# A seventh matmul of 128 rows in place of 96 in the gate/up products of a transformer block

## The chip, the cores and the metric

The kernel runs on one core of a Trainium2 chip. A core has a matrix engine (TensorE, PE in the profile, with its weight loads listed as PEld), a vector engine (DVE), a scalar engine (ACT), a general engine (POOL) and SyncE (SP), which here issues transfers. They run side by side and wait for each other by semaphores. The on-chip memory and the accumulator banks (PSUM) that TensorE writes both have 128 rows (partitions). A matmul takes a stationary operand of up to 128 rows by 128 columns, loaded first, and a moving operand of the same rows and up to 512 columns; the rows are what is summed over. The metric is the time of one execution on the device, in microseconds (us); lower is better.

## The reference

A transformer block on 2048 tokens of width 576: conditioned layer norm, attention with 32 heads of width 18 in four segments of 512 tokens with a running memory, output projection and residual, and then a gated feed-forward part with an inner width of 4608. This case is about the feed-forward part:

```python
def _B_ref(x, w_gate, w_up, w_down):
    g = _silu(x @ w_gate)
    u = x @ w_up
    return (g * u) @ w_down
...
h = _layernorm(x, axis=-1) * (1 + cb) + sb
x = x + gb * _B_ref(h, B_w_gate, B_w_up, B_w_down)
```

## The kernel before

The first part of the kernel (to about 543 us) computes layer norm, projections and attention. The projections to queries and keys (line 576) are chains of 14 matmuls of 128 rows and 512 columns, and the projections to values behind them (line 605) have 288 columns.

The feed-forward part goes through the tokens in two halves (`t` = 0, 1) and in each half through 18 pairs of inner blocks of 128 (`p`, `NPR` = 18). Each product x @ w is made by a Strassen-like scheme: of width, inner block and tokens each halved, seven products of combined operands take the place of eight. So a pair has seven products for the gate (`z` = 0) and seven for up (`z` = 1), 14 in all, and both halves together have 504. Every operand is split into a high and a low part (F32R type), and high x high, low x high and high x low are added.

A half of the width is 288 = 128 + 128 + 32. The function `prod` (lines 1409 to 1417) therefore issues seven matmuls per product: three for each full block of 128, from the weight tiles `wh`, `wl` and the operand tile `y`, and one for the remaining 32. In this seventh one the three combinations of high and low are stacked as 3 x 32 = 96 rows, in the weight tile `R[z]` (called wr in the profile, since its tag is "wr") and in the fifth part of the operand tile, `y[0:96, o, 4]`. The operand tile has room for all seven operands of a half, 128 rows by 7 by 5 by 512.

`prep_r` (lines 1357 to 1366) fills the weight tile: in the first half ACT copies 96 rows (line 1365) and DVE subtracts the low part into rows 32 to 63 (line 1366), in two parts of three and four products; `store_r` keeps the result in memory, and in the second half one transfer brings it back (line 1362). `prep_w` (lines 1376 to 1382) makes wh on ACT and wl on DVE. Before the change the tile is taken anew from the pool `wrp` of two buffers each time, in turns for gate and up. `load_y`, `y_here` and `prep2` write rows 0 to 95 of the fifth part of `y`, never the last 32.

Results of the products gather in three kinds of PSUM banks, A, B and C (`step`), from which ACT and DVE take them (`copy_t`, `fin`). The down projection of the pair before is cut into chunks which run between the products: `down` (line 1525, six matmuls of 288 columns, 14 chunks a pair) in the second half's first 16 pairs, and `plain` (line 1544, twelve matmuls of 288 columns, eight chunks a pair) in all pairs of the first half and the last two of the second. The lists `CH` and `CH0` say at which of the 14 steps a chunk is issued: `CH` has chunks behind 12 steps (behind two of them two chunks) and none behind two, `CH0` has one behind each of eight steps and none behind six. The last eight plain chunks come after all products.

The order of all this is written out by hand: within an engine, instructions run in the order of the program. Ahead of the pairs stands the output projection's last unit (line 874, 32 steps counted by `n`), into which the first preparations are placed: POOL combines weights at steps 2 to 5 (`sum_o`, line 1371), and `prep_r` and `prep_w` stand at the steps listed in `WW`.

Of the kernel before, what the change touches and what calls it, by code (L numbers as in the profile page):

```python
# [8 lines left out]
F32R = mybir.dt.float32r  # L9
# [6 lines left out]
P = 128  # L16
# [83 lines left out]
def f32(ap):  # L100
    return ap.bitcast(F32)
# [3 lines left out]
def block(ctx: ExitStack, tc: tile.TileContext, x, wqk, wv, wo, beta, wgu, wd, c, w_mod, wm01, out):  # L105
    nc = tc.nc
    def pool(stk, name, bufs=1, **kw):
        return stk.enter_context(tc.tile_pool(name=name, bufs=bufs, reuse_waits="tile", **kw))
# [223 lines left out]
    with ExitStack() as p1:  # L332
# [90 lines left out]
        with ExitStack() as p0:  # L423
# [54 lines left out]
            for b in range(3):  # L478
                n = P if b < 2 else 64
# [93 lines left out]
        def proj(s, t):  # L573
            pp = ps.tile([P, L], F32, tag="p", name="pp", bufs=3)
            for n, (a, b) in enumerate(p_ops(s, t)):
                nc.tensor.matmul(pp, lhsT=a, rhs=b, start=(n == 0), stop=(n == 13))
            f = pb.tile([P, L], F32, tag="pf", name="pf")
            fh = pb.tile([P, L], F32R, tag="fh", name="fh")
            fl = pb.tile([P, L], F32R, tag="fl", name="fl")
            nc.scalar.copy(fh, pp)  # L580
            nc.scalar.copy(f, pp)
            nc.vector.tensor_tensor(fl, f, f32(fh), op=ALU.subtract)
            k_store(s, t, fh, fl)
            q_store(s, t, fh, fl)
            q0, q1, r = q_rows(t)
            if q1 > 0:
                if s > 0:
                    e = pb.tile([P, L], F32, tag="pq1", name="pq1")
                    nc.vector.tensor_scalar(e[r:], f[r:], 0.0, None, op0=ALU.min)
                    nc.scalar.activation(e[r:], e[r:], AF.Exp)  # L590
                    nc.vector.scalar_tensor_tensor(e[r:], f[r:], 0.0, e[r:], op0=ALU.max, op1=ALU.add)
                    nc.sync.dma_start(qF[s][q0:q1, :], e[r:])
            return f
# [39 lines left out]
        for s in range(3):  # L633
# [11 lines left out]
            for t in QKORD:  # L645
# [4 lines left out]
                f = proj(s, t)  # L650
# [188 lines left out]
    def load_xr(s, i):  # L839
        xr = o3.tile([P, D], F32, tag="xr", name="xr") if s < 3 or i in (0, 3) else xp.tile([P, D], F32, tag="xs", name="xr")  # L840
        nc.sync.dma_start(xr, x[s][:, i, :])
        return xr

    def wo_r(s, i):
        pt = ps.tile([P, 4, P], F32, tag="b" if s < 3 else "x", name="pto", bufs=8 if s < 3 else 4)
        for kt in range(4):
            nc.tensor.transpose(pt[:, kt, :], ot[s][:, i, 128 * kt:128 * kt + 128], ident)
        pto[s, i] = pt
        oh, ol = [hvp.tile([P, L], F32R, tag=f"{n}{i % 2}", name=n).rearrange("p (a b) -> p a b", b=P) for n in ("hh", "hl")]
        oT[s, i] = (oh, ol, load_xr(s, i) if s < 3 else xr3[i])  # L850

    def wo_s(s, i):
        nc.scalar.copy(oT[s, i][0], pto[s, i])

    def wo_t(s, i):
        oh, ol, _ = oT[s, i]
        nc.vector.tensor_tensor(ol, pto.pop((s, i)), f32(oh), op=ALU.subtract)
# [3 lines left out]
    def wo_m(s, i, h, c):  # L861
        oh, ol, _ = oT[s, i]
        sl = slice(288 * h, 288 * h + 288)
        if c == 0:
            wps[0] = ps.tile([P, L], F32, tag="b" if s < 3 else "w", name="pw", bufs=8 if s < 3 else 2)
        ops = []
        for k in range(4):
            ops += [(oh[:, k], woh[:, k, sl]), (oh[:, k], wol[:, k, sl]), (ol[:, k], woh[:, k, sl])]
        if s == 3:
            ops = [ops[n] for n in (0, 1, 3, 4, 6, 7, 9, 10, 2, 5, 8, 11)]  # L870
        if c == WC - 1:
            ops += [(orr[s][:, i], woh[:, 4, sl]), (orr[s][:, i], wol[:, 4, sl])]
        for n in range(14 * c // WC, 14 * (c + 1) // WC):
            nc.tensor.matmul(wps[0][:, :288], lhsT=ops[n][0], rhs=ops[n][1], start=(n == 0), stop=(n == 13))  # L874

    def wo_x(s, i, h):
        xr = oT[s, i][2]
        sl = slice(288 * h, 288 * h + 288)
        nc.vector.tensor_tensor(xr[:, sl], wps[0][:, :288], xr[:, sl], op=ALU.add)
        if h == 1:  # L880
            (nc.scalar if (s, i) == (2, 3) else nc.sync).dma_start(xD[s][:, i, :], xr)
# [252 lines left out]
    p4 = ExitStack()  # L1134
# [3 lines left out]
    SLOT = {1: 0, 2: 1, 3: 6, 4: 2, 5: 4, 6: 5, 7: 3}  # L1138
    ACT_OP = {1: 0, 2: 1, 3: 2, 4: 6, 5: 3, 6: 4, 7: 5}
# [111 lines left out]
    def y_here(j):  # L1251
        o, kb = (4, 6, 2)[j // 3], j % 3
        n = P if kb < 2 else 96
        f = ys[kb] if o == 4 else yh(1 if o == 6 else 2, kb)
        d = y[:, o, kb if kb < 2 else 4]
        nc.scalar.copy(d[:n], f[:n])
        if kb < 2:
            later.append(lambda: nc.vector.tensor_tensor(y[:, o, 2 + kb], f, f32(d), op=ALU.subtract))
        else:
            later.append(lambda: nc.vector.tensor_tensor(d[64:96], f[64:96], f32(d[64:96]), op=ALU.subtract))  # L1260
# [78 lines left out]
    O, W, R, RW, DP = {}, {}, {}, {}, {}  # L1339
    later = []  # L1340

    def flush():
        while later:
            later.pop(0)()
# [9 lines left out]
    def store_o(p, z, eng=nc.scalar):  # L1354
        eng.dma_start(oD[p][z], O[p, z][:, 3:7, 0:2])

    def prep_r(t, p, z, part=0):
        if part == 0:
            R[z] = wrp.tile([P, 7, P], F32R, tag="wr", name="wr")
        r = R[z]  # L1360
        if t == 1:
            (nc.sync if p or z == 0 else nc.scalar).dma_start(f32(r[0:96]), rD[p][z])
            return
        o, c = O[p, z], slice(0, 3) if part == 0 else slice(3, 7)
        nc.scalar.copy(r[0:96, c], o[0:96, c, 2, :])
        later.append(lambda: nc.vector.tensor_tensor(r[32:64, c], o[32:64, c, 2, :], f32(r[32:64, c]), op=ALU.subtract))

    def sum_o(p, z, j, eng=nc.gpsimd):
        o = O[p, z]
        d, a, b, op = ((4, 3, 2, ALU.add), (5, 4, 0, ALU.subtract), (3, 0, 3, ALU.subtract), (6, 1, 5, ALU.subtract))[j]  # L1370
        eng.tensor_tensor(o[:, d], o[:, a], o[:, b], op=op)  # L1371
# [4 lines left out]
    def prep_w(p, z, m):  # L1376
        o = O[p, z][:, SLOT[m], 0:2]
        wh = wp.tile([P, 2, P], F32R, tag="wh", name="wh")
        wl = wp.tile([P, 2, P], F32R, tag="wl", name="wl")
        nc.scalar.copy(wh, o)  # L1380
        later.append(lambda: nc.vector.tensor_tensor(wl, o, f32(wh), op=ALU.subtract))  # L1381
        W[z, m] = (wh, wl)
# [26 lines left out]
    def prod(z, m, bank, first):  # L1409
        wh, wl = W.pop((z, m))  # L1410
        o = ACT_OP[m]
        ops = [(wh[:, k] if a != 1 else wl[:, k], y[:, o, 2 + k if a == 2 else k])
               for k in range(2) for a in range(3)]
        ops.append((R[z][0:96, SLOT[m]], y[0:96, o, 4]))
        for n, (a, b) in enumerate(ops):
            nc.tensor.matmul(bank, lhsT=a, rhs=b, start=(first and n == 0), stop=(n == 6),  # L1416
                             skip_group_check=not first)
# [169 lines left out]
    with tc.manual_schedule():  # L1587
# [49 lines left out]
        y = yp.tile([P, 7, 5, L], F32R, tag="y", name="y")  # L1637
        tp = pool(p4, "tp")
        opl = pool(p4, "opl")
        wp = pool(p4, "wp", WR)  # L1640
        wrp = pool(p4, "wrp", 2)
        xr3 = {i: load_xr(3, i) for i in range(3)}
        p5 = ExitStack()
        ys = [hvp.tile([P, L], F32, tag="hh2", name="ys"), yt[2][:, 4, :L],
# [19 lines left out]
        for i in range(4):  # L1664
            for h in range(2):
                for c in range(WC):
                    n = 8 * i + 4 * h + c
                    wo_m(3, i, h, c)
                    if c == 3:
                        wo_x(3, i, h)  # L1670
                    flush()
                    if n in SS:
                        j = SS.index(n)
                        sum_o(0, j // 4, j % 4, nc.vector if j > 3 else nc.gpsimd)
                    if n == 24:
                        nc.scalar.activation(omg[:, 0:1], omg[:, 0:1], AF.Silu)
                        store_o(0, 0)
                    if n in HH:
                        y_here(HH.index(n))
                    if n in WW:  # L1680
                        j = WW.index(n)
                        if j < 2:
                            prep_r(0, 0, 0, j)
                        prep_w(0, 0, next(gw))
                if h == 1 and i < 2:
                    wo_r(3, i + 2)
                    wo_s(3, i + 2)
                    wo_t(3, i + 2)
# [14 lines left out]
        n, nw = 0, PF  # L1703
# [5 lines left out]
        for t in range(2):  # L1709
            for p in range(NPR):  # L1710
# [16 lines left out]
                for k in range(14):  # L1727
                    z, m = ZM[PRIME[k] if prev is None else k]
# [66 lines left out]
                    if prev is not None and is_plain(*prev):  # L1795
# [3 lines left out]
                        if CH0[t][k]:  # L1799
                            f = plain(*prev, chunk)  # L1800
# [103 lines left out]
```

## Time and profile before

| | |
|---|---|
| median of 3 runs | 1809.43 us |
| lowest and highest | 1808.07 and 1813.18 us |
| the profiled execution, first to last instruction | 1808.8 us |
| TensorE busy | 1783.9 us, 99% |
| weight loads busy | 1512.5 us, 84% |
| DVE busy | 1485.3 us, 82% |
| ACT busy | 947.8 us, 52% |
| POOL busy | 493.5 us, 27% |
| first and last start of a gate/up matmul | 543.6 and 1791.4 us |

The profile shows one execution. Of that execution no time beside its span was kept, so the median of the runs, 0.6 us above the span, stands for what lies around it. Matmuls are pipelined: the next one starts while the one before is still shown as running, and the shown ends are modelled. The distance from start to start says how long a matmul holds the engine; the shown duration is longer. In a row, "A<-y,wr 96*128 96x512" is a matmul that writes the bank A from the operand y and the weights wr, with a stationary operand of 96 rows by 128 columns and a moving one of 96 rows by 512 columns. "x288" is a count. What stands behind "<-" in a wait is what ended it.

### The profile page before, as it was taken

How to read it: one execution, taken by the hardware profiler on the slowest of the kernel's cores; microseconds unless marked ns; L12 is line 12 of the kernel's file. 1: busy time of each engine (PE TensorE's matmuls, PEld its weight loads, DVE VectorE, ACT ScalarE, POOL GpSimd, SP SyncE). 2: the span in 40 equal slices, each digit the busy share in tenths (PEclk: the TensorE clock that was granted, in tenths of full speed). 3: DMA queues.
4: the chain of work that ended last, by engine and by line, in shares of the span. 5: the costliest groups of instructions: out<-in, count | busy, mean ns of one | idle time of the engine just before them, and what ended most of it. 6: DMA issues, size and time to landing. Idle time of an engine off the chain costs nothing.

```text
span 1808.8 us, 31104 instructions
## 1 busy us (share of the span) xinstructions
PE 1783.9 (99%) x11053; PEld 1512.5 (84%) x11053; DVE 1485.3 (82%) x3278; ACT 947.8 (52%) x2073; POOL 493.5 (27%) x707
## 2 busy tenths in 40 slices
PE   8999999999999999999999999999999999999999
PEld 5888867767777888888888888888888888888888
DVE  7567589999978888889889897768888888888886
ACT  6344578778865445445544444344544544544542
POOL 2100146556661545544455444100000000000000
PEclk9999999999999999999999999999999999999999
DMA  8678766677677555456554544683324324323331
GB/s 296 225 242 281 235 200 178 173 194 217 185 236 258 174 197 173 147 169 208 170 158 141 169 147 135 199 282 130 107 80 129 107 82 128 108 82 128 107 103 53
DMA packets 178562, 304.49 MB, mean 168 GB/s; under 512 B 25304, under 2 KB 108184, under 8 KB 176616
## 3 DMA queue, kind: packets, MB, share of 16 engines
q1 hardware_dynamic: 151032, 248.66, 44.0%
q10 hardware_dynamic: 27376, 53.86, 8.5%
q8 instruction: 87, 1.43, 0.3%
q14 instruction: 67, 0.55, 0.1%
HBM read 188.42 MB, written 113.33 MB: 167 GB/s over the span
## 4 chain that ended last, share of the span: by engine, by line
PE 78%; DMA 3%; DVE 3%; POOL 1%; issue 1%; ACT 1%; ACTq 0%; SPq 0%; POOLq 0%; DVEq 0%
PE A L1416 24%; PE pd L1544 14%; PE C L1416 12%; PE pd L1525 10%; PE B L1416 6%; PE av L766 3%; PE pw L874 2%; PE s L711 2%; PE s L740 2%; PE pn L1010 1%; DMA y<-yD 1%; DVE junk L211 1%; DMA O<-in_wgu_dram 1%; DMA xD<-xr 1%; PE pw L951 1%
## 5 line engine op out<-in xcount | busy, mean ns | idle before, releaser
L1416 PE MATMUL A<-y,wh 128*128 128x512 f32 x1152 | 406.2, 393 | 2.3 <-DMA y<-yD 1.4
L1416 PEld LDWEIGHTS A<-y,wh 128*128 128x128 f32 x1152 | 216.6, 188 | 47.3 <-ACT B L1462 2.4
L1381 DVE TENSOR_TENSOR wl<-O,wh 128x256 fp32r<-128x256 f32 x504 | 246.4, 494 | 2.1 <-ACT wh L1380 1.6
L211 DVE CUSTOM_DVE_ANT_0 junk<-s,tri 128x384 bf16<-128x384 f32 (+3 forms) x512 | 218.5, 486 | 22.7 <-PE s L711 8.8
L1416 PE MATMUL A<-y,wl 128*128 128x512 f32 x576 | 226.9, 394 | 0.0
L1530 DVE TENSOR_TENSOR acc<-acc,pd 128x576 f32<-128x576 f32 x216 | 162.1, 751 | 59.2 <-PE pd L1525 51.6
L1416 PE MATMUL C<-y,wh 128*128 128x512 f32 x576 | 202.9, 393 | 1.5 <-DVE cu L1439 1.5
L1380 ACT CAST wh<-O 128x256 fp32r<-128x256 f32 x504 | 197.7, 405 | 4.9 <-DMA yD<-st 3.0
L1554 DVE TENSOR_TENSOR acc<-acc,pd 128x576 f32<-128x576 f32 x156 | 116.9, 749 | 89.0 <-PE pd L1544 88.3
L1544 PE MATMUL pd<-dh,ah 128*128 128x288 f32 x640 | 189.0, 295 | 0.5 <-DVE x L1548 0.5
L1544 PE MATMUL pd<-dh,al 128*128 128x288 f32 x640 | 189.1, 296 | 0.0
L1544 PE MATMUL pd<-dl,ah 128*128 128x288 f32 x640 | 188.8, 295 | 0.0
L1371 POOL TENSOR_TENSOR O<-O 128x384 f32<-128x384 f32 x132 | 149.4, 1145 | 142.7 <-DMA O<-in_wgu_dram 60.6
L1485 ACT CAST ah<-sg 128x512 fp32r<-128x512 f32 x192 | 119.1, 621 | 75.6 <-DVE sg L1440 69.3
L747 ACT ACTIVATE Pt<-s 128x512 f32<-128x512 f32 x256 | 135.4, 599 | 21.8 <-PE s L740 11.6
L1486 DVE TENSOR_TENSOR al<-sg,ah 128x512 fp32r<-128x512 f32 x192 | 136.3, 710 | 9.9 <-ACT ah L1485 9.7
L1525 PE MATMUL pd<-dh,ah 128*128 128x288 f32 x448 | 133.0, 297 | 0.0
L1525 PE MATMUL pd<-dh,al 128*128 128x288 f32 x448 | 132.5, 296 | 0.0
L1525 PE MATMUL pd<-dl,ah 128*128 128x288 f32 x448 | 132.3, 295 | 0.0
L1416 PEld LDWEIGHTS C<-y,wh 128*128 128x128 f32 x576 | 108.3, 188 | 22.3 <-DVE cu L1439 1.9
L1544 PEld LDWEIGHTS pd<-dl,ah 128*128 128x128 f32 x640 | 120.5, 188 | 7.2
L1544 PEld LDWEIGHTS pd<-dh,ah 128*128 128x128 f32 x640 | 120.8, 189 | 6.8 <-DVE x L1548 0.8
(412 smaller groups left out, 4337.2 us busy)
## 6 DMA issues: line engine op xcount, KB each, us to landing
O<-in_wgu_dram SPq DMA_DIRECT2D x36, 768.0 KB
O<-oD SPq DMA_DIRECT2D x36, 512.0 KB
oD<-O ACTq DMA_DIRECT2D x34, 512.0 KB
ks<-kD SPq DMA_DIRECT2D x64, 216.0 KB
qs<-qD SPq DMA_DIRECT2D x64, 216.0 KB
O<-in_wgu_dram SPq DMA_DIRECT2D x36, 384.0 KB
rD<-wr ACTq DMA_DIRECT2D x36, 336.0 KB
wr<-rD SPq DMA_DIRECT2D x35, 336.0 KB
```

Source lines behind the costliest of these rows:

```text
L211: nc.vector.tensor_tensor_reduce(junk[:, :n], bank[:, o:o + n], tri[:, L - n:], 1.0, -3e38, op0=ALU.add, op1=ALU.max, accum_out=mcol[u][0] ...
L747: nc.scalar.activation(pt[:, h], bank, AF.Exp, scale=SCALE)
L1371: eng.tensor_tensor(o[:, d], o[:, a], o[:, b], op=op)
L1380: nc.scalar.copy(wh, o)
L1381: later.append(lambda: nc.vector.tensor_tensor(wl, o, f32(wh), op=ALU.subtract))
L1416: nc.tensor.matmul(bank, lhsT=a, rhs=b, start=(first and n == 0), stop=(n == 6), skip_group_check=not first)
L1485: nc.scalar.copy(ah, src)
L1486: later.append(lambda: nc.vector.tensor_tensor(al, src, f32(ah), op=ALU.subtract))
L1525: nc.tensor.matmul(pd[:, i, :288], lhsT=a[:, tk], rhs=w, start=(k == 0), stop=(k == 2))
L1530: nc.vector.tensor_tensor(o, o, pd[:, :, :288], op=ALU.add)
L1544: nc.tensor.matmul(pd[:, i, :288], lhsT=a[:, tk], rhs=w, start=(k == 0), stop=(k == 5))
L1554: nc.vector.tensor_tensor(o, o, pd[:, :, :288], op=ALU.add)
```

## The change

The seventh matmul of a product reads all 128 rows of the weight tile and of the operand. The last 32 rows of both are zero, so the sums are the same. For that the two weight tiles, one for gate and one for up, are made once, when the pool is opened, and no longer taken anew for each pair; POOL writes zeros into their rows 96 to 127, and into rows 96 to 127 of the fifth part of `y` for all seven operands. These nine memsets stand at step 6 of the output projection's last unit, behind the four weight sums on POOL. All later writers touch rows 0 to 95 alone.

```diff
     def prep_r(t, p, z, part=0):
-        if part == 0:
-            R[z] = wrp.tile([P, 7, P], F32R, tag="wr", name="wr")
         r = R[z]
...
-        ops.append((R[z][0:96, SLOT[m]], y[0:96, o, 4]))
+        ops.append((R[z][:, SLOT[m]], y[:, o, 4]))
...
-        wrp = pool(p4, "wrp", 2)
+        wrp = pool(p4, "wrp")
+        for z in range(2):
+            R[z] = wrp.tile([P, 7, P], F32R, tag=f"wr{z}", name=f"wr{z}")
...
+                    if n == 6:
+                        for z in range(2):
+                            nc.gpsimd.memset(f32(R[z][96:128]), 0.0)
+                        for o in ACT_OP.values():
+                            nc.gpsimd.memset(f32(y[96:128, o, 4]), 0.0)
```

## The prediction

> **What bounds the kernel now.** I read the page first (part 1, then the chain of part 4), then the waits of the last 1266 us, then windows, then one matmul line.
>
> Part 1, the engines, and part 4, the chain by engine and by line:
>
> ```profile
> PE 1783.9 (99%) x11053; PEld 1512.5 (84%) x11053; DVE 1485.3 (82%) x3278; ACT 947.8 (52%) x2073; POOL 493.5 (27%) x707
> ...
> PE 78%; DMA 3%; DVE 3%; POOL 1%; issue 1%; ACT 1%; ACTq 0%; SPq 0%; POOLq 0%; DVEq 0%
> PE A L1416 24%; PE pd L1544 14%; PE C L1416 12%; PE pd L1525 10%; PE B L1416 6%; PE av L766 3%; PE pw L874 2%; PE s L711 2%; PE s L740 2%; PE pn L1010 1%; DMA y<-yD 1%; DVE junk L211 1%; DMA O<-in_wgu_dram 1%; DMA xD<-xr 1%; PE pw L951 1%
> ```
>
> All waits of the matmul queue from 543 us, where the gate/up products begin, to the end (total, times, longest, in us):
>
> ```profile
> PE C L1416 <- DVE cu L1439: 1.5, 1, 1.5
> PE A L1416 <- DMA y<-yD: 1.4, 1, 1.4
> PE A L1416 <- ACT B L1462: 0.9, 3, 0.3
> PE pd L1544 <- DVE x L1548: 0.5, 1, 0.5
> ```
>
> Two windows of that stage, one in each token half (length, then busy time and count of PE, weight loads, DVE, ACT, POOL, then granted clock, DMA share, GB/s):
>
> ```profile
> 600.00:700.00 100.00, 100.00 (x551) 87.89 (x550) 83.09 (x137) 48.97 (x110) 50.18 (x49) 1.00 0.53 174
> 1400.00:1500.00 100.00, 100.00 (x540) 87.59 (x539) 85.86 (x159) 48.30 (x112) 0.00 (x0) 1.00 0.35 107
> ```
>
> TensorE waits 4.3 us in 1266 and never stops inside either window; the clock is granted in full. So in this stage the end is set by the distance from one matmul's start to the next one's, which I call the step. A nanosecond off a step is a nanosecond off the run as long as DVE, 86 us busy in 100, keeps up.
>
> **Where the steps are long.** Line 1416 by its groups (min/median/max ns, first and last start):
>
> ```profile
> L1416 PEld LDWEIGHTS A<-y,wh x1152: 186/188/192, 543.4 to 1789.4; 128*128 128x128 f32 x192
> L1416 PE MATMUL A<-y,wh x1152: 387/389/504, 543.6 to 1789.6; 128*128 128x512 f32 x192
> ...
> L1416 PEld LDWEIGHTS A<-y,wr x288: 187/188/188, 544.7 to 1789.6; 96*128 96x128 f32 x144
> L1416 PE MATMUL A<-y,wr x288: 391/397/403, 544.9 to 1789.8; 96*128 96x512 f32 x144
> ...
> L1416 PE MATMUL C<-y,wr x144: 391/397/402, 549.8 to 1791.4; 96*128 96x512 f32 x144
> ...
> L1416 PE MATMUL B<-y,wr x72: 391/397/402, 546.6 to 1783.4; 96*128 96x512 f32 x72
> L1416 PEldq EVENT_SEMAPHORE  x7: 51/51/51, 540.1 to 1191.4; - x7
> ```
>
> The 96-row matmul occurs 288 + 144 + 72 = 504 times, the last of seven in each product. It lasts 397 ns in the median, the commonest 128-row one 389: 8 ns more. The ends are modelled, so I check by starts. First a stretch in which all matmuls have 128 rows, the q/k projections of the first stage: timeline of TensorE (start us, us), then a window of that line with its count:
>
> ```profile
> 41.39 0.39 PE L576 MATMUL pp<-hh,wqkl 128*128 128x512 f32 x1
> 41.61 0.39 PE L576 MATMUL pp<-hl,wqkh 128*128 128x512 f32 x1
> ...
> 49.32 0.29 PE L605 MATMUL pv<-wvh,hh 128*128 128x288 f32 x1
> ...
> 50.11 0.29 PE L605 MATMUL pv<-wvh,hh 128*128 128x288 f32 x1
> ...
> 50.90 0.29 PE L605 MATMUL pv<-wvh,hr 128*128 128x288 f32 x1
> ```
>
> ```profile
> 41.62:49.31 7.69, 7.69 (x35) 6.19 (x33) 1.00 0.88 292
> ```
>
> 35 matmuls touch the window; the one of 41.39 began before it, so 34 begin from 41.61 until the 288-column one at 49.32: 7.71 / 34 = 227 ns a step, kept over products that end and new PSUM banks that begin (each projection is 14 matmuls). Call this the settled step. Six, then twelve matmuls of 288 columns behind it take 0.79 and 1.58 us.
>
> Now products that follow each other directly in the stage at issue:
>
> ```profile
> 707.90 0.40 PE L1416 MATMUL C<-y,wr 96*128 96x512 f32 x1
> ...
> 709.52 0.40 PE L1416 MATMUL A<-y,wr 96*128 96x512 f32 x1
> ...
> 717.58 0.40 PE L1416 MATMUL A<-y,wr 96*128 96x512 f32 x1
> ```
>
> The first seven-matmul product takes 1.62 us, and six take 9.68 us: 1613 ns each. Seven settled steps are 7 x 226.8 = 1587. So 26 ns of every chained product are lost, and of the shapes in it only the seventh's row count differs from the projections.
>
> Last, products with down-projection matmuls (288 columns) between them:
>
> ```profile
> 903.95 0.30 PE L1544 MATMUL pd<-dh,ah 128*128 128x288 f32 x1
> ...
> 905.54 0.40 PE L1416 MATMUL A<-y,wh 128*128 128x512 f32 x1
> ...
> 906.92 0.40 PE L1416 MATMUL A<-y,wr 96*128 96x512 f32 x1
> ```
>
> ```profile
> 1504.57 0.30 PE L1525 MATMUL pd<-dh,ah 128*128 128x288 f32 x1
> ...
> 1505.37 0.39 PE L1416 MATMUL A<-y,wh 128*128 128x512 f32 x1
> ...
> 1506.76 0.40 PE L1416 MATMUL A<-y,wr 96*128 96x512 f32 x1
> 1506.99 0.30 PE L1525 MATMUL pd<-dh,ah 128*128 128x288 f32 x1
> ...
> 1507.80 0.39 PE L1416 MATMUL B<-y,wh 128*128 128x512 f32 x1
> ```
>
> Behind a 96-row matmul twelve 288-column ones take 1.59 us (settled 1.58), six take 0.80 and 0.81 (settled 0.79): some 10 and 15 ns more a run. The six 512-column steps after such a run are also slow: 1.38 and 1.39 us, against 6 x 0.2268 = 1.36.
>
> **The change part by part.**
>
> *The seventh matmul at 128 rows: its own step.* 504 x 8 ns (397 against 389) = 4.0 us saved. All on the path, since TensorE is what ends last.
>
> *The products that follow directly.* The lists of down chunks put work behind 12 of 14 products for 16 pairs and behind 8 of 14 for 19 pairs: 344 products. Of the other 160, a dozen stand before transposes, so about 148 run into the next product. They lose 26 ns each, of which 8 are counted: 148 x 18 = 2.7 us.
>
> *The down runs.* 344 runs, 10 to 15 ns each. Only one stretch shows how such a run goes behind settled 128-row matmuls, so the bounds are 0 and 344 x 15 = 5.2. I take 12 ns, 4.1 us, since that stretch has the same two shapes in the same order.
>
> *The steps after a down run.* 20 to 30 ns each, by the rows at 905.54 and 1505.37. Between those 288-column matmuls and these 512-column ones the row count doesn't change, only the columns do, and no row shows this passage without a 96-row matmul shortly ahead. Bounds: 0, and 344 x 22 = 7.6 us. I take 0, because the change leaves this passage as it is.
>
> *The load of 128 rows for 96.* 188 ns either way in the rows above, beside the running matmul: 0. A loss is excluded as long as the load is no longer than that of the other six.
>
> *Nine memsets on POOL at step 6 of the last output-projection unit.* The rows: POOL's last work before the stage and its next, the copy on ACT that waits for POOL there, and a memset of 512 columns:
>
> ```profile
> 532.63 1.19 POOL L1371 TENSOR_TENSOR O<-O 128x384 f32<-128x384 f32 x1
> 576.80 1.44 POOL L1394 TENSOR_TENSOR dr__9005<-dr__9005,gbB 128x576 f32<-128x576 f32 x1 [42.97 <-DMA dr__9005<-in_wd_dram]
> ```
>
> ```profile
> 533.86 0.62 ACT L1365 CAST wr<-O 96x512 fp32r<-96x512 f32 x1 [4.02 <-POOL O L1371]
> ```
>
> ```profile
> L148 POOL MEMSET tri<- 128x512 f32 x1 | 0.5, 519 | 0.0
> ```
>
> Seven of 512 columns and two of 896 (at 519 / 512 ns a column, 0.9 us each) are 5.4 us. They queue behind the four sums that end at 533.82 and end at about 539.2. POOL has nothing else until 576.8, and the first seventh matmul starts at 544.94 (the row group above gives 544.9): 5.7 us to spare, so 0. If the copy at 533.86 had to wait for them too, it would come 5.4 us later and cost 0 to 5.4 us of the end; I take 0, as it writes rows 0 to 95 and the memsets rows 96 to 127.
>
> *Two fixed weight tiles in place of a rotating pair.* The copies write the same two buffers in the same turn, after the same readers; with 0 idle time of the matmul queue on these tiles there is nothing to gain, and ACT (48 us in 100) would hide a later copy: 0.
>
> Sum: 4.0 + 2.7 + 4.1 = 10.8 us off the span of 1808.8, giving 1798.0. The median of the runs, 1809.4, stands 0.6 above that span, so the time is **1798.6 us**.
>
> **The rivals.**
>
> *Rows don't matter (0.13).* The 8 ns could belong to the place (the last matmul of a product, with stop set and someone waiting), not to the rows. For it: both loads take 188 ns. Against it: projections also stop every 14 matmuls, and the 34 steps from 41.61 pass two such ends at 227 ns. Time: no term left, 1809.4. The Trainium skill has a rule to this effect ("TensorE: Matmul & The Clock Gate", section "LDWEIGHTS (loading the stationary operand)"): a load of 32 rows takes as long as one of 128, since only the columns count. The equal 188 ns agree with it, the steps don't follow from it; by the rule alone the change would be worth nothing.
>
> *Only the own step (0.06).* The 8 ns go, but each product still starts unsettled because of its waits on new weights. 4.0 us: 1805.4.
>
> *The passage from down runs settles too (0.10).* Then the last bound is added: 10.8 + 7.6 = 18.4, 1791.0. For it: at 905.54 and 1505.37 the slow steps differ with what went before; against it: a change of columns remains.
>
> *TensorE gets ahead of its feeders (0.04).* With 1% less TensorE time DVE is 86.7 us busy in 100, and a chain from bank to operands could come late. Against it: 4.3 us of waits in 1266 now. If half the gain is lost: 1804.0.
>
> *A semaphore instruction per product (0.05), the slower side.* The seventh matmul now reads rows of two writers in each operand. If that gives it one wait more than it can carry, the queue gets an extra semaphore instruction like the seven in the last row of line 1416, 51 ns each, where the load ahead of it stands: 504 x 51 = 25.7 less 10.8 gained, 1824.3. It decides from 212 products on (10.8 us / 51 ns). Against it: POOL writes these rows once, before the stage, so one wait covers all later reads.
>
> **How the numbers follow.** Forecast 0.62. Its own range is 1793 to 1803 (the down runs at 0 to 5.2, and part of the passage). Reaching to 1791.0 and 1805.4 takes in 0.62 + 0.10 + 0.06 + 0.04 = 0.82, so the range is 1790 to 1806. What a measurement can tell from no change is about 0.3%, 5.4 us: faster is below 1804.0. Faster: the forecast, the larger gain and half the feeder case, 0.74; same: 0.13 + 0.06 + 0.02 = 0.21; slower 0.05.
>
> **What will show it.** Right: the groups of line 1416 that read wr have 128 rows and a median near 389; chained products are 1.59 us apart; the first six steps of a down run take 0.79; the window of 1400 holds about 545 matmuls instead of 540. Wrong: the median of these groups stays at 397 with 128 rows (the place, not the rows), new semaphore rows on the matmul queue at this line, or waits of TensorE well over 4.3 us. If the products shorten and the runs don't, the step that failed is the 12 ns a run.

## The result and the profile after

The changed kernel takes 1799.22 us in the median of 6 runs (1798.3 to 1805.54), beside 1809.37 us for the kernel before in the same comparison: 0.994 of it, 95% interval 0.9929 to 0.9952. Line numbers of the feed-forward part are two lower than before (1414 for 1416, 1523 for 1525, 1542 for 1544).

Part 1 and part 4 of the page of the changed kernel (span 1796.9 us), and then all waits of its matmul queue from the first product on:

```profile
PE 1772.0 (99%) x11053; PEld 1507.2 (84%) x11053; DVE 1487.7 (83%) x3278; ACT 948.4 (53%) x2073; POOL 498.3 (28%) x716
...
PE 78%; DVE 4%; DMA 2%; POOL 1%; issue 1%; ACT 1%; ACTq 0%; SPq 0%; POOLq 0%; DVEq 0%
```

```profile
PE A L1414 <- DMA y<-yD: 1.1, 1, 1.1
PE A L1414 <- ACT B L1460: 1.0, 3, 0.5
PE C L1414 <- DVE cu L1437: 0.6, 1, 0.6
PE pd L1542 <- DVE x L1546: 0.5, 1, 0.5
PE A L1414 <- ACT tb L1443: 0.5, 1, 0.5
```

TensorE still sets the end: it is busy 11.9 us less, the span is 11.9 us shorter, and its waits are 3.7 us where they were 4.3. Nothing else has become late. Of the 11.9 us, 0.9 lie ahead of the stage that was changed (the first matmul of a product starts at 542.7 instead of 543.6); the other 11.0 are the stage's own.

Where in the stage did it go? Two matmuls of the second token half, in each kernel the same one of the program, twelve pairs of inner blocks apart, and in between the window of the tile wr alone, with its count of matmuls and of weight loads (the two x168). First the kernel before:

```profile
1284.02 0.40 PE L1416 MATMUL C<-y,wr 96*128 96x512 f32 x1
...
1690.74 0.40 PE L1416 MATMUL C<-y,wr 96*128 96x512 f32 x1
```

```profile
1284.00:1690.70 406.70, 66.75 (x168) 31.53 (x168) 0.00 (x0) 0.00 (x0) 1.00 0.34 106
```

and the changed kernel:

```profile
1276.55 0.39 PE L1414 MATMUL C<-y,wr 128*128 128x512 f32 x1
...
1679.67 0.39 PE L1414 MATMUL C<-y,wr 128*128 128x512 f32 x1
```

168 products are 12 pairs of 14. A pair takes 406.72 / 12 = 33.893 us before and 403.12 / 12 = 33.593 us after: 300 ns saved. The prediction's terms come to 12 x (8 + 12) + 2 x 26 = 292 ns for such a pair. This length is the sharper measure in what follows, since it does not contain the part ahead of the products, whose end moves from execution to execution. (The changed kernel itself was profiled twice: the first product starts at 542.7 us in one trace and at 547.4 in the other.)

Inside a pair the gain does not lie where the prediction put it. Line 1414 by groups (min/median/max ns), the seventh matmuls (wr), and above them those of bank A that read wl, the second and fifth of a product:

```profile
L1414 PE MATMUL A<-y,wl x576: 387/389/398, 542.9 to 1777.5; 128*128 128x512 f32 x192
...
L1414 PE MATMUL A<-y,wr x288: 388/396/398, 544.1 to 1778.0; 128*128 128x512 f32 x144
...
L1414 PE MATMUL C<-y,wr x144: 388/393/398, 548.8 to 1779.5; 128*128 128x512 f32 x144
...
L1414 PE MATMUL B<-y,wr x72: 388/396/396, 545.7 to 1771.6; 128*128 128x512 f32 x72
L1414 PEldq EVENT_SEMAPHORE  x10: 51/51/51, 540.3 to 1184.7; - x10
```

The wl row in the kernel before:

```profile
L1416 PE MATMUL A<-y,wl x576: 387/395/402, 543.8 to 1789.4; 128*128 128x512 f32 x192
```

The seventh matmuls are still at 393 to 396 in the median (397 before), not at 389. But the matmuls that read wl have come from 395 to 389: the gain has moved from the seventh matmul to the ones that follow in the next product. The timeline of TensorE in the changed kernel shows the same: a run of twelve with the first six matmuls of the product behind it, and three chained products; then the same of a product between two runs of six:

```profile
699.29 0.30 PE L1542 MATMUL pd<-dh,ah 128*128 128x288 f32 x1
...
700.88 0.39 PE L1414 MATMUL A<-y,wh 128*128 128x512 f32 x1
...
702.24 0.40 PE L1414 MATMUL A<-y,wr 128*128 128x512 f32 x1
...
705.42 0.39 PE L1414 MATMUL C<-y,wr 128*128 128x512 f32 x1
...
710.18 0.39 PE L1414 MATMUL C<-y,wr 128*128 128x512 f32 x1
```

```profile
1493.53 0.40 PE L1414 MATMUL C<-y,wh 128*128 128x512 f32 x1
...
1494.91 0.39 PE L1414 MATMUL C<-y,wr 128*128 128x512 f32 x1
...
1495.95 0.39 PE L1414 MATMUL A<-y,wh 128*128 128x512 f32 x1
```

Three chained products take 4.76 us, 1587 ns each, as forecast (1613 before). The run of twelve takes 1.59 us as before, but the six steps behind it are settled: 1.36 us instead of 1.38. The product between the runs of six is still at 1.38 in its first six steps (over all of them the mean has come down too, as the section on the prediction shows), and its seventh matmul with the run behind it (1494.91 to 1495.95) at 1.04 us, as before (1506.76 to 1507.80).

The rest of the prediction's signs: the window from 1400 to 1500 us holds 543 matmuls (540 before, 545 forecast), and the memsets ran where they were placed, behind the four sums:

```profile
1400.00:1500.00 100.00, 100.00 (x543) 87.83 (x542) 86.85 (x162) 49.23 (x114) 0.00 (x0) 1.00 0.33 105
```

```profile
534.53 1.63 POOL L1677 MEMSET wr<- 32x896 f32 x2
536.10 3.33 POOL L1679 MEMSET y<- 32x512 f32 x7
```

They take 4.9 us (5.4 forecast) and end at 539.43, and the first seventh matmul starts at 544.1.

### The profile page after: what moved, and what is told of

The parts are those of the page before. It is cut to its first block, busy times and chain, and to the rows that moved or that the text cites. A ratio compares the mean times of both kernels' runs of the same rounds, so it can differ in the third digit from the quotient of the medians.

```text
span 1796.9 us, 31117 instructions
## 1 busy us (share of the span) xinstructions
PE 1772.0 (99%) x11053; PEld 1507.2 (84%) x11053; DVE 1487.7 (83%) x3278; ACT 948.4 (53%) x2073; POOL 498.3 (28%) x716
## 4 chain that ended last, share of the span: by engine, by line
PE 78%; DVE 4%; DMA 2%; POOL 1%; issue 1%; ACT 1%; ACTq 0%; SPq 0%; POOLq 0%; DVEq 0%
PE A L1414 24%; PE pd L1542 13%; PE C L1414 12%; PE pd L1523 10%; PE B L1414 6%; PE av L766 3%; PE pw L874 2%; PE s L711 2%; PE s L740 2%; PE pn L1010 1%; DMA y<-yD 1%; PE pw L951 1%; DVE junk L211 1%; PE px L788 1%; DVE wl L1379 1%
## 5 line engine op out<-in xcount | busy, mean ns | idle before, releaser
L1379 DVE TENSOR_TENSOR wl<-O,wh 128x256 fp32r<-128x256 f32 x504 | 251.2, 504 | 2.1 <-ACT wh L1378 1.6
```

## The experiments

Theory: among 512-column matmuls TensorE keeps a settled step of 227 ns as long as consecutive ones use the same number of rows; a change of the count (128 to 96 and back) unsettles it for about four steps, some 26 ns in all. Rivals: 96 rows are slow as such; the place at the end of a product is slow, whatever its rows; the fixed tiles bring the gain.

Pair lengths below are worked out as above, from the same two matmuls of each trace. Single steps and means without a row of their own come from the starts of all matmuls of the trace named. Times are medians; the ratio is to the kernel before on the same chip.

### The tiles without the rows

```diff
-        ops.append((R[z][:, SLOT[m]], y[:, o, 4]))
+        ops.append((R[z][0:96, SLOT[m]], y[0:96, o, 4]))
```

> The changed kernel with its two fixed weight tiles and its nine memsets, but the seventh matmul again reads rows 0 to 95 alone. Theory (the change of the row count from 128 to 96 and back lengthens the steps): the time of before, 1809.4 us within 2, median duration of the 96-row matmuls 397 ns, chained products 1613 ns. Rival (fixed tiles or the place of the preparations bring the gain): 1799 us.

1811.2 us, ratio 1.0009 (0.9996 to 1.0021): the time of before.

```profile
1283.55 0.40 PE L1414 MATMUL C<-y,wr 96*128 96x512 f32 x1
...
1690.27 0.40 PE L1414 MATMUL C<-y,wr 96*128 96x512 f32 x1
```

Over twelve pairs 406.72 us, the same to the hundredth as before. Fixed tiles and memsets are worth nothing by themselves; the rows are all of it.

### 128 rows in the gate products alone

```diff
+        n7 = 128 if z == 0 else 96
-        ops.append((R[z][:, SLOT[m]], y[:, o, 4]))
+        ops.append((R[z][0:n7, SLOT[m]], y[0:n7, o, 4]))
```

> The changed kernel with 128 rows in the seventh matmul of the gate products (252) and 96 rows in that of the up products (252). Theory: half of the 10.2 us, 1804.3 us within 1.5; the wr groups split into a median near 389 to 392 at 128 rows and 397 at 96. Rival (one 96-row matmul now and then keeps the stream unsettled throughout): 1807 or more.

1807.06 us, ratio 0.9981 (0.9972 to 0.999).

```profile
1286.47 0.40 PE L1415 MATMUL C<-y,wr 96*128 96x512 f32 x1
...
1691.67 0.40 PE L1415 MATMUL C<-y,wr 96*128 96x512 f32 x1
```

405.20 / 12 = 33.767 us a pair: 127 of the 300 ns. The median lies outside the forecast 1804.3 within 1.5 and at the rival's 1807; the ratio is a gain of 0.2%, where all seventh matmuls padded gave 0.6. The pair length, which does not contain the part ahead, says more: half of the seventh matmuls padded, 42% of the gain. What decides against the rival are products that follow each other directly, here two of the gate:

```profile
552.31 0.39 PE L1415 MATMUL B<-y,wr 128*128 128x512 f32 x1
...
553.90 0.39 PE L1415 MATMUL A<-y,wr 128*128 128x512 f32 x1
```

They are 1.59 us apart, settled, though the next products of up are disturbed: the median of all starts is 1587 ns for a padded product behind a padded one and 1614 for a 96-row one behind a 96-row one. The other expected sign failed: the medians of the wr durations are 396 ns at 128 rows and 397 at 96, which can't be told apart.

### The 96-row matmul in the fourth place

```diff
-        ops.append((R[z][0:96, SLOT[m]], y[0:96, o, 4]))
+        ops.insert(3, (R[z][0:96, SLOT[m]], y[0:96, o, 4]))
```

> The kernel before with the 96-row matmul as the fourth of seven, the last one being a 128-row matmul. Theory (rows): the long steps move with it: the 96-row matmul itself about 233 ns, the three behind it 237, 233 and 231, chained products still about 1613 ns, and the seventh, now of 128 rows, shorter in the median than 397; time between 1801 and 1812 us. Rival (place: the last matmul of a product is slow, whatever its rows): the seventh keeps 397 ns, the fourth is at 389, time 1809.4 us.

1811.25 us, ratio 1.0002 (0.9993 to 1.0011). The groups of the wh and wr matmuls in bank A, and then the two matmuls of the pair length:

```profile
L1416 PE MATMUL A<-y,wh x1152: 388/395/507, 548.4 to 1792.1; 128*128 128x512 f32 x192
...
L1416 PE MATMUL A<-y,wr x288: 392/395/470, 549.1 to 1791.4; 96*128 96x512 f32 x144
```

```profile
1285.40 0.39 PE L1416 MATMUL C<-y,wr 96*128 96x512 f32 x1
...
1692.28 0.39 PE L1416 MATMUL C<-y,wr 96*128 96x512 f32 x1
```

406.88 / 12 = 33.907 us, 13 ns more than before. The median of the wh matmuls has gone from 389 to 395: the long steps have moved to the matmuls behind the 96-row one, as the theory says. In its chained products the starts of all matmuls of the trace give 232 or 233 ns for the fourth step, then 237, 233 and 231, then 227 three times, and their sum is 1613 as before. The seventh step ahead of a run is at 235 (237 before), so it hardly became shorter; that expectation failed, and the section on the prediction comes back to it. The time alone could not have told theory and rival apart.

### 96 rows everywhere

All seven matmuls and all down-projection matmuls of the stage use rows 0 to 95; rows 96 to 127 of the two full blocks and of the down projection's inner block are left out of the sums.

```diff
-        ops = [(wh[:, k] if a != 1 else wl[:, k], y[:, o, 2 + k if a == 2 else k])
+        ops = [(wh[0:96, k] if a != 1 else wl[0:96, k], y[0:96, o, 2 + k if a == 2 else k])
...
-                nc.tensor.matmul(pd[:, i, :288], lhsT=a[:, tk], rhs=w, start=(k == 0), stop=(k == 2))
+                nc.tensor.matmul(pd[:, i, :288], lhsT=a[0:96, tk], rhs=w[0:96], start=(k == 0), stop=(k == 2))
...
-                    nc.tensor.matmul(pd[:, i, :288], lhsT=a[:, tk], rhs=w, start=(k == 0), stop=(k == 5))
+                    nc.tensor.matmul(pd[:, i, :288], lhsT=a[0:96, tk], rhs=w[0:96], start=(k == 0), stop=(k == 5))
```

> The kernel before with all seven matmuls of every product and all down-projection matmuls at rows 0 to 95 (rows 96 to 127 of the two full blocks and of the down projection's inner block are left out of the sums). Nothing changes its row count inside the stage. Theory (it is the change of count that costs): as fast as the changed kernel, 1799.2 us within 2, chained products 1587 ns. Rival (a 96-row matmul is slow as such, 233 to 237 ns a step): products of 7 x 235 = 1645 ns or more, 504 x 32 ns = 16 us above before, 1825 us.

1801.69 us, ratio 0.9949 (0.9936 to 0.9961).

```profile
1281.01 0.39 PE L1416 MATMUL C<-y,wr 96*128 96x512 f32 x1
...
1684.12 0.39 PE L1416 MATMUL C<-y,wr 96*128 96x512 f32 x1
```

403.11 / 12 = 33.593 us a pair, that of the changed kernel, and chained products at 1587 ns. 96 rows are as fast as 128; it is the change of count that costs. This is the run that settles the matter: the rival with 16 us more is out.

### Four changes in a product

The fourth matmul also reads 96 rows only; 32 rows of the second full block are left out of one of its three terms.

```diff
         ops.append((R[z][0:96, SLOT[m]], y[0:96, o, 4]))
+        ops[3] = tuple(v[0:96] for v in ops[3])
```

> The kernel before with the fourth matmul of every product at rows 0 to 95 too (32 rows of the second full block are left out of one of its three terms), so that the row count changes four times in a product instead of twice. Theory (each change costs): some 20 ns more in each of 504 products, 1815 to 1824 us, chained products near 1635 ns. Rival (96 rows cost a fixed amount by themselves): refuted already by the kernel with 96 rows throughout if that stays at 1587 ns; it would give 504 x 8 ns, 1814 us at most.

1814.84 us, ratio 1.0021 (1.0009 to 1.0033).

```profile
1286.38 0.40 PE L1417 MATMUL C<-y,wr 96*128 96x512 f32 x1
...
1694.94 0.40 PE L1417 MATMUL C<-y,wr 96*128 96x512 f32 x1
```

408.56 / 12 = 34.047 us, 153 ns more than before, 11 ns for each of 14 products, where 20 were expected; the median lies just under the forecast range. The time alone would also fit the rival's 1814. Products that follow each other directly tell the two apart:

```profile
710.15 0.40 PE L1417 MATMUL C<-y,wr 96*128 96x512 f32 x1
...
711.78 0.40 PE L1417 MATMUL A<-y,wr 96*128 96x512 f32 x1
```

They are 1.63 us apart, in the median of all starts 1633 ns, where the rival would give 1613 + 8 = 1621: here the full 20 ns were paid. The rest is missing at the down runs. Behind a run of six the six steps became 16 ns longer in the mean, but the seventh step and the run itself 3 and 1 ns shorter; why, no run shows.

### 64 rows

The seventh matmul reads rows 0 to 63; 32 rows (high x low of the narrow block) are left out.

```diff
-        ops.append((R[z][0:96, SLOT[m]], y[0:96, o, 4]))
+        ops.append((R[z][0:64, SLOT[m]], y[0:64, o, 4]))
```

> The kernel before with the seventh matmul at rows 0 to 63 (the 32 rows of high x low of the narrow block are left out). Theory A (any change of the row count costs what 96 costs): 1809.4 us within 2. Theory B (64 rows belong to another size of the array's rows, as the 54- and 56-row score matmuls of the attention part do, where the step at the passage is 319 to 338 ns instead of 227): about 90 + 100 ns in each of 504 products, 1905 us.

1997.67 us, ratio 1.1025 (1.1004 to 1.1046). The step into such a matmul, its own and the one behind it, and the two of the pair length:

```profile
1389.16 0.40 PE L1416 MATMUL C<-y,wh 128*128 128x512 f32 x1
1389.48 0.50 PE L1416 MATMUL C<-y,wr 64*128 64x512 f32 x1
1389.91 0.40 PE L1525 MATMUL pd<-dh,ah 128*128 128x288 f32 x1
1390.15 0.29 PE L1525 MATMUL pd<-dl,ah 128*128 128x288 f32 x1
...
1860.68 0.50 PE L1416 MATMUL C<-y,wr 64*128 64x512 f32 x1
```

The step ahead takes 0.32 us and its own 0.43, where settled ones take 0.227; the first step of the run behind it takes 0.24 us, where settled 288-column ones take 0.13. Together that is some 400 ns. The pair takes 471.20 / 12 = 39.267 us: (39.267 - 33.893) / 14 = 384 ns more in a product than 96 rows cost. Theory B had the right kind and half the size. So there are two prices: 26 ns for 96 rows, some 400 for 64. The Trainium skill ("TensorEngine Tiling (Array Packing)", section "Tiling Modes") says that a change of the tiling mode drains the TensorE, and lists modes of 128, 64 and 32 rows; the rows above agree with it for 64. That 96 rows stay within the mode of 128 would fit their small price, but no row here shows it.

### 96 rows in the products, 128 in the down runs

The rows 96 to 127 of the two full blocks are left out of the products; the down projection is whole.

```diff
-        ops = [(wh[:, k] if a != 1 else wl[:, k], y[:, o, 2 + k if a == 2 else k])
+        ops = [(wh[0:96, k] if a != 1 else wl[0:96, k], y[0:96, o, 2 + k if a == 2 else k])
```

> The kernel before with all seven matmuls of every product at rows 0 to 95 (the last 32 rows of the two full blocks are left out), the down-projection matmuls at 128 rows. The row count changes only at the 344 down runs. Theory: chained products 1587 ns as in the changed kernel; about 20 ns for each of the 344 runs and the product behind it, 1799.2 + 7 = 1806 us (1803 to 1809). Rival (the place of the last matmul): 1809.4 us.

1805.05 us, ratio 0.9966 (0.9954 to 0.9979), within the forecast.

```profile
1281.99 0.40 PE L1416 MATMUL C<-y,wr 96*128 96x512 f32 x1
...
1685.43 0.40 PE L1416 MATMUL C<-y,wr 96*128 96x512 f32 x1
```

But 20 ns at every passage did not come; two very different sizes did. In the second half a pair takes 403.44 / 12 = 33.620 us, only 27 ns over the changed kernel for twelve passages with a change of count: 2 ns each. There a run of six became 4 ns longer in the mean and the six steps behind it 4 ns shorter. In the first half, where the runs have twelve matmuls, a passage costs more than the forecast:

```profile
721.45 0.30 PE L1544 MATMUL pd<-dh,ah 128*128 128x288 f32 x1
...
724.43 0.40 PE L1416 MATMUL A<-y,wr 96*128 96x512 f32 x1
```

From the start of the run to the seventh matmul behind it this is 2.98 us, where the changed kernel's rows above have 2.95 (699.29 to 702.24); the medians of the first half are 34 ns apart, 14 in the run and 20 in the six steps behind it. From the first product to the last matmul the trace is 3.9 us longer than the changed kernel's, about half of the 7 forecast. Why the two kinds of run differ stays open.

### Fewer passages

```diff
-CH = (1, 1, 1, 1, 2, 1, 0, 1, 1, 1, 1, 2, 1, 0)
+CH = (0, 2, 0, 2, 2, 0, 2, 0, 2, 0, 2, 0, 2, 0)
```

This is the changed kernel with its six-matmul chunks issued two at a time.

> The changed kernel with the 14 down chunks of a pair in seven groups of two (in the 16 pairs that use six-matmul chunks), so that a pair has seven passages from products to 288-column matmuls and back instead of twelve. Theory (what is left of the unsettled steps sits at these passages, some 25 ns each): 16 x 5 = 80 passages fewer, 2.0 us off, 1797.2 us. Rival (the passages are free now): 1799.2 us; if DVE comes late with two chunks in a row, more than 1799.2.

1799.52 us, ratio 0.9928 (0.9912 to 0.9945): by the median the rival's 1799.2, but the kernel before took 1811.19 us on this chip, 1.8 more than beside the changed kernel. The next comparison therefore has the changed kernel, this one and a third that also groups the twelve-matmul chunks side by side on one chip:

> The changed kernel once more, beside the two grouped ones on the same chip: ratio to before 0.9944, first product to last matmul 1250.7 us within 1.5.

> The changed kernel with seven groups of two down chunks a pair, again. Theory (some 25 ns for each of the 80 passages saved, the same stretch 3.5 us shorter in the first look at it): 2 to 3.5 us faster than the changed kernel of the same call, ratio to before about 0.993. Rival: no difference, the first look's stretch was chance.

```diff
-CH0 = ((0, 0, 0, 0, 1, 1, 1, 1, 1, 1, 1, 1, 0, 0), (0, 0, 0, 1, 1, 1, 1, 1, 1, 1, 1, 0, 0, 0))
+CH0 = ((0, 0, 0, 0, 0, 2, 0, 2, 0, 2, 0, 2, 0, 0), (0, 0, 0, 0, 2, 0, 2, 0, 2, 0, 2, 0, 0, 0))
...
-                        if CH0[t][k]:
+                        for q in range(CH0[t][k]):
```

> The same, and the eight twelve-matmul chunks of the other 19 pairs in four groups of two: 76 passages fewer. These passages already end settled in the changed kernel (226 ns behind the run), so only the 6 ns ahead of the run and 3 ns in its first steps are left: 0.7 us less than with seven groups alone, within what can be told. Rival (25 ns as at the other runs): 1.9 us less.

The changed kernel: 1802.06 us, ratio 0.9952 (0.9939 to 0.9965), and 1251.1 us from its first product to its last matmul. Chunks of six grouped: 1799.99, 0.9932 (0.992 to 0.9944). Both grouped: 1799.03, 0.9935 (0.9922 to 0.9949). The intervals overlap, so the times alone do not show a gain over the changed kernel. The pair length does; the changed kernel's second trace and the first grouped one:

```profile
1281.69 0.39 PE L1414 MATMUL C<-y,wr 128*128 128x512 f32 x1
...
1684.81 0.39 PE L1414 MATMUL C<-y,wr 128*128 128x512 f32 x1
```

```profile
1276.28 0.40 PE L1414 MATMUL C<-y,wr 128*128 128x512 f32 x1
...
1677.40 0.40 PE L1414 MATMUL C<-y,wr 128*128 128x512 f32 x1
```

403.12 us again for the changed kernel, 401.12 for the grouped one: 167 ns a pair, 33 for each of the five passages saved (25 expected), and 16 x 0.167 = 2.7 us over the pairs that have such chunks (2.0 to 3.5 expected). Chunks of six in groups of two are therefore faster than the changed kernel, by 2.7 us of these pair lengths and 2.1 of the medians. Grouping the twelve-matmul chunks as well brought nothing that can be told (0.7 us expected).

## Why the prediction came out right

The forecast was 1798.6 us, the time is 1799.22. Step by step; the measured sizes without a row above come from the starts of all matmuls in the two traces (before and after), matched one for one from the first product on and summed by place:

- **TensorE's steps set the end.** Right: 11.9 us less busy time of TensorE, 11.9 us less span, waits of 3.7 us instead of 4.3. DVE at 86.85 us in 100 kept up, as at 86.7 forecast.
- **Chained products, 26 ns each.** Right: 1613 to 1587 ns. What was forecast beyond the seventh's own step, 2.7 us, is 3.0 in the sum.
- **The seventh matmul's own step, 8 ns at all 504.** Mis-sized. Where a product follows it falls by 6 ns in the median, from 233 to 227; where a run follows, only by about 5, from 237 to 232. The sum over all 504 is 2.3 us instead of 4.0. The prediction read 8 ns off the medians of two groups of modelled durations, 397 against 389, and expected the seventh to join the other group. The group stayed at 393 to 396.
- **The down runs, 12 ns each, 4.1 us.** Mis-sized. A run of six became 3 ns shorter in the mean (799 to 796), one of twelve in the first half 3 ns in the median (1591 to 1588), and only the 32 double runs of the second half (two chunks of six issued together) 20 ns. Weighted by their counts, (160 x 3 + 152 x 3 + 32 x 20) / 344 = 5 ns, 1.6 us. The stretch of the projections from which the 12 ns came passes from 512 to 288 columns without the 5 ns that the products keep ahead of a run, so it was not the same passage, though its shapes were. A run of six still takes 796 ns where the projections' first six take 787: most of its excess did not come from the rows.
- **The steps after a down run, taken as 0.** Mis-sized the other way. The truth lay midway between the two bounds: behind a run of twelve in the first half the first three steps 234, 236, 227 became 226, 227, 227, 20 ns over six steps in the median and 13 in the mean, and behind a run of six 14 ns of the mean are gone. In sum 160 x 14 + 127 x 13 = 3.9 us; behind the double runs and the few plain runs of the second half there is next to nothing. The reason for taking 0, that the change leaves this passage as it is, was wrong: these steps depended on the rows of the matmul ahead of the run, six or twelve matmuls earlier. The kernels with fixed tiles alone (234, 236 behind a run of twelve) and with 96 rows throughout (226, 227) show the same.
- **Load, memsets, fixed tiles at nothing.** Right: the experiment with the tiles alone repeats the pair length of before to the hundredth.

So the bound and the cause were right (the change of rows lengthens steps, and TensorE's steps set the end), the places only in part, and the total is that close by luck: 4.2 us too much (2.5 at the runs, 1.7 at the seventh steps) met 4.2 too little (3.9 behind the runs, 0.3 in the chained products). The four sums, 2.3 + 3.0 + 1.6 + 3.9 = 10.8 us, agree with the 11.0 us by which the stage became shorter from its first product to its last matmul; the medians of the runs are 10.2 apart.

Of the rivals, "rows don't matter" falls with the kernel of 96 rows throughout and the one with fixed tiles alone: count unchanged, fast; count changed, slow. The equal times of the loads on which it rested are still there (188 ns at 128 rows as at 96), so the cost of a change of rows isn't in the load's time. "Only the own step" falls with the chained products. "The passage settles too" was right about the place, but it brought 3.9 of its 7.6 us, and what the runs were to bring was missing. The feeder rival falls with the waits of 3.7 us. The semaphore rival falls with the count of such instructions at this line, ten instead of seven, where it would take some 504.

What stays open: why the step ahead of a down run is 232 ns in the changed kernel and in the one with 96 rows throughout, when the projections show 227 ns in the same passage from 512 to 288 columns. No run here varied what differs between them (the first matmul of a run needs fresh operands and a freed bank), so this is not settled. Open too is why a change of count at a passage costs 34 ns with a run of twelve and 2 with a run of six, and in what the disturbance consists; the runs show when it comes and what it costs.

## What to carry to other kernels

When TensorE is the bound and its waits are near nothing, compare the distance from start to start with that of the longest undisturbed stretch in the same trace; durations of pipelined matmuls mix a matmul's own share with that of its neighbours (the wl matmuls here went from 395 to 389 ns without a change of their own). In this stage 512-column matmuls of one row count, all 128 or all 96, kept their shortest step when they followed each other directly; so it is worth trying to pad a narrow rest of a contraction with zero rows kept in place rather than to run it at its own row count, as long as the rows are free to have. And a term that is bounded from both sides with no row for the value deserves its middle rather than an end: 0 was taken of 0 to 7.6 us, and 3.9 came.

## What the runs showed of the hardware that was not expected

- 96 rows throughout are as fast as 128, to the hundredth of a microsecond (403.11 and 403.12 us for twelve pairs); one matmul of 96 rows among 128-row ones of 512 columns costs 26 ns, 6 in its own step and 20 in the three behind it.
- 64 rows among 128 cost some 400 ns: 0.32 us for the step ahead, 0.43 us for its own and 0.11 us more for the one behind, 186 us in the whole kernel (1997.67 against 1811.19).
- A 96-row matmul ahead of a run of twelve 288-column matmuls shows in the product 1.59 us later: its first two steps were 234 and 236 ns, and 226 and 227 with 128 rows there.
- A change of count where the columns change too has no one price: 34 ns around a run of twelve, 2 around a run of six.
- The twelve pairs repeat themselves to the hundredth of a microsecond from execution to execution (403.12 us twice in the changed kernel), while the spans of these two executions, 1796.9 and 1802.1 us, differ by some 5 us, and 4.8 of these lie ahead of the first product.
